# A rewritten order of work up to block d in a fused SSD and squared-ReLU kernel

## The chip, the core and the metric

One core of a Trainium2 chip runs the whole program. Its engines are TensorE (PE), VectorE (DVE), ScalarE (ACT), GpSimd (POOL) and SyncE (SP); each takes its instructions strictly in the order in which the kernel lists them for it. SP, ACT and POOL also issue the transfers between HBM and the core's memory. The metric is the device time of one execution in microseconds (us). The kernel before took 117.4 us, the median of three runs (115.73 to 117.66).

## What is computed

The first part is a chunked state-space recurrence over 4 batches, 8 heads, 768 steps, 32 channels and a state of 16; the second is a feed-forward layer on its result, seen as 3072 tokens of 256 features.

```python
cum = np.cumsum(log_a, axis=-1)                  # in a chunk of 32 steps
L = np.exp(cum[..., :, None] - cum[..., None, :]) * causal
M = np.einsum('bhin,bhjn->bhij', Cc, Bc) * L
y = np.einsum('bhij,bhjd->bhid', M, xc) + np.einsum('bhin,bhnd->bhid', Cc, state) * np.exp(cum)
state = exp(sum(la)) * state + sum_j(B_j x_j exp(cum[-1] - cum_j))
...
h = np.maximum(x @ w_in, 0.0)                    # w_in 256 x 2048
out = (h * h) @ w_out                            # w_out 2048 x 256
```

## The kernel before, in words

The work is cut into 12 units, one for each of 4 batches (b) and 3 stretches of 256 steps (j). Units 0 to 3 are the first stretches of the four batches; units 4 to 11 go on from their states. The result of unit k is a tile `T` of 256 tokens, and block a is the feed-forward layer on unit 0's tokens, block b on unit 1's, and so on to l.

Every step is a token of a hand-written list, `ORDER`, and each engine's queue is simply the order in which the tokens call it. A digit behind the name is the unit, a letter after a colon the engine (`v` DVE, `a` ACT, `p` POOL, `s` SP). The tokens that matter here:

- `id3:512`: three products on constant ones, 512 columns wide (L476), with no use but to keep TensorE busy. `fa`, `la`: the loads of the first and of the later part of `a`. `ldC1:s`, `ldB1:s`, `ldx1:s`: loads of a unit's inputs; `ld4` all three. `wi0` to `wi3`, `wo0` to `wo3`: the weights, a quarter each, cast on the way by POOL's queue (L139, L143). `gB3`: a one-element memset by POOL into the tile of B3, so that the load of B3, and what stands behind it on SP, waits for POOL to come by.
- `sk`, `sp`, `sn`, `p2`: the running products of `a` (clip and scan on DVE, L468 and L469; products on TensorE, L452) for the first and for the later stretches. `pc`, `pb`, `px`: scale C, copy B into the tile `jt`, scale x (L158, L168 or L170, L177). `tr`, `tc`: transpose `jt` on TensorE and copy it back (L195, L208); from unit 4 on `tr` is a transposing transfer issued by SP (L186).
- `mt`: 16 products that give the scores of a unit in PSUM banks 0 to 3 (L220). `mk`: mask one bank on DVE (L229). `sc`: copy one bank on ACT (L234), and `ms` masks that copy on POOL or DVE (L238). `u`: the states (L245), `us` their copy, `z` and `s` (`za`, `sa`, ...) their running sum and its spread form; `sf` is that for the first stretches (L343). `in`, `ina`, `inb`: masked scores times x; `ca`: state times C; `t`: copy of the result to `T`. `rg4` does all of these for a pair of neighbouring units at once.
- `a0` to `a7`: block a's eight first products, each four matmuls and a relu on ACT (L403, L408). `qa0`: the square on DVE (L414). `A0` to `A7`: the second products, four matmuls each into an accumulating bank (L430); the last one is followed by a copy on ACT and a store on SP (L437, L438).

PSUM has eight banks. Six of them go round: the helper `bank()` takes the next in `turn` that is not in `busy`, so which bank a token gets, and whose earlier content must be read before it may write, follows from the list. A first product, a transpose, a unit's states and the scores all draw on these six.

Before, the front is: fillers of 512 columns, `a`, x0, B0, C0, and the loads of units 1 to 3 one behind the other on SP without a pause, since `gB3` stands near the start. The weights come in the order `wi0 wi1 wo0 wi2 wi3 wo1 wo2 wo3`. Blocks a, b and c are mixed with each other and with the units: four first products come before `A0`, products of a and b are still left when unit 3 and block c begin, and 14 groups of products stand between `rg4` and `rg5`.

Of the kernel before, what the change touches and what calls it, by code (L numbers as in the profile page):

```python
# [30 lines left out]
def kernel(  # L31
# [77 lines left out]
    pp = psum.tile([128, 8, 512], FP32, name="pp")  # L109

    def total(i, b, j):
        return 4 * i + b if j == 0 else 8 + 8 * (j - 1) + 4 * i + b
# [223 lines left out]
        else:  # L336
            state[b] = (z, S_d)

    def ph_sd_first(k):
# [3 lines left out]
        nc.vector.tensor_tensor(  # L343
            out=_fap(S_d, 0, [[128, 2], [32, 4], [1, 32]]),
            in0=_fap(pp, v["h"][0] * 512 + 256, [[32, 2], [0, 4], [1, 32]]),
            in1=_fap(Pquad, 4 * total(0, b, 0), [[0, 2], [1, 4], [0, 32]]), op=ALU.mult)
# [87 lines left out]
    def ph_out(blk):  # L434
        b, j = UNITS[blk]
        osb = opool.tile([128, 512], FP32, tag="osb", name=f"osb{blk}")
        nc.scalar.copy(out=osb, in_=pp[:, 6 if blk == 1 else 7, :])  # L437
# [18 lines left out]
    with tc.manual_schedule():  # L456
# [198 lines left out]
        def one(t):  # L655
            f = t.split(":")
            name = f[0].rstrip("0123456789")
            k = int(f[0][len(name):] or 0)
# [13 lines left out]
            {  # L672
                "a": lambda: None,
                "fa": lambda: first_a(k, eng),
                "la": late_a,
                "ldC": lambda: load(k, "C", eng, f[1] if len(f) > 2 else None),
                "ldB": lambda: load(k, "B", eng, f[1] if len(f) > 2 else None),
                "ldx": lambda: load(k, "x", eng, f[1] if len(f) > 2 else None),
                "ld": lambda: load_all(k),
                "gC": lambda: gate(k, "C"), "gB": lambda: gate(k, "B"), "gx": lambda: gate(k, "x"),  # L680
                "afC": lambda: after("C", k), "afB": lambda: after("B", k), "afx": lambda: after("x", k),
                "wi": lambda: load_w_in(k), "wo": lambda: load_w_out(k),
                "id": lambda: idle(k, f[1], dep(f[2]) if len(f) > 2 else None),
                "ef": lambda: eye(eye_f, ones_f), "eb": lambda: eye(eye_b, ones_b[:, 0:128]), "wm": warmed, "hd": head_rows,
                "jz": lambda: eng.memset(jt[k], 0.0), "ti": triangle, "pi": picks, "ku": quads,
                "mb": causal, "pk": picked, "sk": lambda: scan(0), "sp": first_p, "sn": second_scan,
                "su": first_sums, "to": first_total, "fq": first_quad, "p": lambda: second_p(), "pq": second_quad,
                "ps": lambda: A.copy(out=P_sb[:, :, 0:32], in_=P0.rearrange("p (r c) -> p r c", r=2)),  # L688
                "iv": lambda: inv(int(f[1]), int(f[2]), k == 1),
                "pc": lambda: prep_c(k, eng or P, P0 if k == 0 else None),  # L690
                "pb": lambda: prep_b(k, eng or P), "pbl": lambda: prep_b(k, eng, (0,)), "pbh": lambda: prep_b(k, eng, (1,)),
                "px": lambda: prep_x(k, eng or P),
                "tr": lambda: transpose(k, "") if k < 4 else dma_tr(k),
                "trC": lambda: transpose(k, "C"), "trB": lambda: transpose(k, "B"),
                "tc": lambda: trc(k, "", f[1], eng), "tcC": lambda: trc(k, "C", f[1], eng), "tcB": lambda: trc(k, "B", f[1], eng),
                "mt": lambda: scores(k), "mk": lambda: mask_direct(k) if k < 4 else next_mask(k), "sc": lambda: score_copy(k),
                "ms": lambda: mask_copied(k, eng),
                "u": lambda: first_u(k, f[1] if len(f) > 1 else None), "sf": lambda: ph_sd_first(k),
                "ca": lambda: ph_carry(k, live[k]["h"], live[k]["begun"]),
                "in": lambda: intra(k, ""), "ina": lambda: intra(k, "a"), "inb": lambda: intra(k, "b"),  # L700
                "t": lambda: region_t(k, f[1]), "us": lambda: region_us(k),
                "rg": lambda: rg(k), "bk": late_banks, "fr": lambda: busy.discard(4),
                "za": lambda: ph_z(k, 0), "zb": lambda: ph_z(k, 1), "sa": lambda: ph_sd(k, 0), "sb": lambda: ph_sd(k, 1),
            }[name]()
# [59 lines left out]
```

## Time and profile before

| what | value |
|---|---|
| median of three runs | 117.4 us |
| the profiled execution's own time | 116.84 us |
| its span | 115.1 us |
| TensorE busy | 108.9 us, 95% |
| DVE busy | 84.2 us, 73% |
| ACT busy | 76.7 us, 67% |
| POOL busy | 49.8 us, 43% |

The times below are counted from the start of the span. A row of a timeline gives start, length, engine, line, operation, output and inputs, how many were merged, and in brackets how long the engine stood idle before it and what ended that. Lengths of TensorE products overlap, so the distance between starts says more than the length.

### The profile page before, as it was taken

How to read it: one execution, taken by the hardware profiler on the slowest of the kernel's cores; microseconds unless marked ns; L12 is line 12 of the kernel's file. 1: busy time of each engine (PE TensorE's matmuls, PEld its weight loads, DVE VectorE, ACT ScalarE, POOL GpSimd, SP SyncE). 2: the span in 40 equal slices, each digit the busy share in tenths (PEclk: the TensorE clock that was granted, in tenths of full speed). 3: DMA queues.
4: the chain of work that ended last, by engine and by line, in shares of the span. 5: the costliest groups of instructions: out<-in, count | busy, mean ns of one | idle time of the engine just before them, and what ended most of it. 6: DMA issues, size and time to landing. Idle time of an engine off the chain costs nothing.

```text
span 115.1 us, 3998 instructions
## 1 busy us (share of the span) xinstructions
PE 108.9 (95%) x1623; PEld 93.5 (81%) x1623; DVE 84.2 (73%) x187; ACT 76.7 (67%) x161; POOL 49.8 (43%) x102
## 2 busy tenths in 40 slices
PE   7977969999999999999999999999999999999990
PEld 2344749978898989989989989989989899899980
DVE  2469996779599969969965989849668488445530
ACT  0655667865598756787486686786777776876840
POOL 7369972068599457548602669038020020000000
PEclk9999999999999999999999999999999999999999
DMA  1999999989999913935915926623023020020202
GB/s 29 199 196 145 199 203 189 215 167 210 180 191 211 214 24 108 160 89 155 179 46 122 178 97 123 132 95 73 0 100 68 0 100 0 6 91 0 91 0 91
DMA packets 47814, 13.46 MB, mean 117 GB/s; under 512 B 44276, under 2 KB 45876, under 8 KB 47796
## 3 DMA queue, kind: packets, MB, share of 16 engines
q1 hardware_dynamic: 43828, 10.64, 44.8%
q0 software_dynamic: 1664, 2.10, 10.8%
q10 hardware_dynamic: 2304, 0.48, 2.0%
q8 instruction: 12, 0.20, 0.8%
q14 instruction: 6, 0.05, 0.1%
HBM read 10.58 MB, written 3.15 MB: 119 GB/s over the span
## 4 chain that ended last, share of the span: by engine, by line
PE 87%; DMA 6%; POOL 2%; issue 1%; DVE 1%; ACT 1%; ACTq 0%; DVEq 0%
PE pp L430 36%; PE pp L403 36%; PE pp L245 6%; DMA w_out_b<-in_moe_w_out_dram 6%; PE pp L476 4%; PE pp L220 3%; POOL mts L238 1%; PE pp L195 1%; POOL jt L158 1%; PE pp L452 1%; DVE jt L158 0%; DVE Sd L343 0%; ACT bct L208 0%; PE pp L521 0%; ACT osl L722 0%
## 5 line engine op out<-in xcount | busy, mean ns | idle before, releaser
L408 ACT ACTIVATE hb<-pp 128x512 bf16<-128x512 f32 x96 | 55.0, 599 | 24.7 <-PE pp L403 23.1
L430 PE MATMUL pp<-w_out_b,h 128*128 128x256 bf16 (+1 forms) x400 | 54.3, 268 | 0.8 <-DMA w_out_b<-in_moe_w_out_dram 0.8
L414 DVE TENSOR_TENSOR h<-hb 128x512 bf16<-128x512 bf16 x96 | 45.0, 486 | 12.7 <-ACT hb L408 12.3
L403 PE MATMUL pp<-T,w_in_b 128*128 128x256 bf16 x384 | 54.2, 273 | 0.0
L403 PEld LDWEIGHTS <-w_in_b 128*128 128x128 bf16 x384 | 41.4, 114 | 2.2 <-issue 1.0
L430 PEld LDWEIGHTS <-h 128*128 128x128 bf16 x400 | 37.6, 98 | 5.4 <-DVE T L210 1.1
L229 DVE TENSOR_TENSOR mts<-pp,mask 128x512 bf16<-128x512 f32 x45 | 29.6, 677 | 3.3 <-PE pp L220 3.3
L331 POOL TENSOR_TENSOR Sd<-z,Pquad 128x256 bf16<-128x256 f32 x16 | 11.1, 693 | 32.9 <-DVE z L315 25.7
L177 POOL TENSOR_TENSOR xs<-x_nat,Pinv 128x256 bf16<-128x256 f32 (+1 forms) x19 | 14.4, 776 | 5.2 <-DVE Pinv L546 4.6
L158 POOL TENSOR_TENSOR jt<-C_nat,P_sb 128x128 bf16<-128x128 f32 x22 | 9.4, 449 | 1.5 <-ACT P_sb L688 1.0
L476 PE MATMUL pp<-const-bfloat16-1.0 128*128 128x512 bf16 (+2 forms) x19 | 7.3, 516 | 0.8 <-PEq L748 0.8
L315 DVE SCALAR_TENSOR_TENSOR z<-z,Ptot,us 128x64 f32<-128x64 f32 x8 | 2.2, 281 | 6.3 <-ACT us L299 5.4
L437 ACT COPY osb<-pp 128x512 f32<-128x512 f32 x11 | 6.3, 584 | 0.4 <-PE pp L430 0.4
L245 PE MATMUL pp<-mts,xs 64*32 64x128 bf16 x384 | 5.9, 219 | 0.1
L170 POOL CAST jt<-B_nat 128x128 bf16<-128x128 f32 x17 | 5.4, 341 | 1.4 <-DMA B_nat<-in_B_dram 1.4
L220 PE MATMUL pp<-bct 32*64 32x256 bf16 x192 | 5.1, 279 | 0.9 <-DVE bct L210 0.6
L476 PEld LDWEIGHTS <-const-bfloat16-1.0 128*128 128x128 bf16 x19 | 2.2, 122 | 4.0 <-issue 3.7
L245 PEld LDWEIGHTS <-xs 64*32 64x32 bf16 x384 | 4.2, 90 | 0.6 <-issue 0.4
L282 ACT CAST T<-pp 128x512 bf16<-128x512 f32 x7 | 4.1, 592 | 0.4 <-PE pp L245 0.2
L208 ACT CAST T<-pp 128x256 bf16<-128x256 f32 x8 | 2.6, 375 | 2.6 <-PE pp L245 2.6
L245 PE MATMUL pp<-bct,Sd 128*128 128x128 bf16 x40 | 4.2, 220 | 0.0
L220 PEld LDWEIGHTS <-bct 32*64 32x64 bf16 x192 | 2.1, 102 | 2.0 <-issue 0.6
(62 smaller groups left out, 53.4 us busy)
## 6 DMA issues: line engine op xcount, KB each, us to landing
x_nat<-in_x_dram SPq DMA_DIRECT2D x11, 256.0 KB, 3.7
out_dram<-osb SPq DMA_DIRECT2D x11, 256.0 KB, 3.2
B_nat<-in_B_dram SPq DMA_DIRECT2D x11, 128.0 KB, 3.1
C_nat<-in_C_dram SPq DMA_DIRECT2D x11, 128.0 KB, 3.4
w_in_b<-in_moe_w_in_dram POOLq DMA_DIRECT2D x4, 256.0 KB, 6.8
w_out_b<-in_moe_w_out_dram POOLq DMA_DIRECT2D x4, 256.0 KB, 8.2
x_nat<-in_x_dram ACTq DMA_DIRECT2D x2, 128.0 KB, 3.4
bct<-jt SPq DMA_TRANSPOSE x8, 3.6
```

What stands on the lines that cost most here:

```text
L158: eng.tensor_tensor(out=_fap(jt[k % 3], 128 + 144 * g, [[384, 2], [32, 4], [1, 16]]), in0=_fap(loaded[k]["C"], 128 * g, [[16, 2], [32, 4], ...
L177: eng.tensor_tensor(out=_fap(xs, 256 * r, [[256, 2 // n], [32, 8], [1, 32]]), in0=_fap(loaded[k]["x"], 32 * r, [[32, 2 // n], [64, 8], [1, ...
L220: nc.tensor.matmul(pp[64 * u:64 * u + 64, q, r * 256:r * 256 + 256], bct[32 * q:32 * q + 32, r, 0, u * 64:u * 64 + 64], _fap(bct[32 * q:32 ...
L229: nc.vector.tensor_tensor(out=live[k]["mts"][:, q].rearrange("p r g i -> p (r g i)"), in0=pp[:, q, :], in1=mask, op=ALU.mult)
L245: nc.tensor.matmul(dst, w, v, start=bool(need), stop=False, skip_group_check=True, **({} if pos is None else {"tile_position": pos}))
L331: nc.gpsimd.tensor_tensor(out=_fap(S_d, 0, [[128, 2], [32, 4], [1, 32]]), in0=_fap(z, 0, [[32, 2], [0, 4], [1, 32]]), in1=_fap(Pquad, 4 * ...
L403: nc.tensor.matmul(pp[:, h, i * 256:(i + 1) * 256], _fap(w, g * w.shape[2] + (o // 2) * 512 + 2 * (o % 2) + i, [[4, 128]]), T[blk][:, g].r ...
L408: nc.scalar.activation(out=hb.rearrange("p i t -> p (i t)"), in_=pp[:, h, :], func=AF.Relu)
L414: nc.vector.tensor_tensor(out=h2, in0=hb, in1=hb, op=ALU.mult)
L430: nc.tensor.matmul(dst, h2[:, i, r * 128:(r + 1) * 128], w_out_b[gi][:, 2 * o + i, c0:c1], start=first, stop=(fp == 7 and i == 1), skip_gr ...
L437: nc.scalar.copy(out=osb, in_=pp[:, 6 if blk == 1 else 7, :])
L476: nc.tensor.matmul(pp[:, h, 0:int(cols)], ones_b[:, 0:128], ones_b[:, 0:int(cols)] if dep is None else dep, start=True, stop=True, skip_gr ...
```

## The change

The list is rewritten up to the token `D0`; from there on it is unchanged. In the new list `a`, C0, B0 and x0 are loaded in this order, then unit 1, then the later part of `a`. The fillers are 128 columns wide, 51 in all, 24 of them ahead of the first real product. Weights come in turn: `wi0 wo0 wi1 wo1 wi2 wo2 wi3 wo3`. B2 is gated behind `wo2`, B3 behind `wo3`. Unit 1 has two of its four scores copied by ACT, like unit 0, and not masked straight from PSUM. `sf0` and `sf1` become four ACT instructions each. The products of a and b follow one another in their natural order, those of c come after all of a and b, and six groups stand between `rg4` and `rg5`.

```diff
     ORDER = """
-        id3:512 fa1:a la fa0:s ku ef ldx0:h:a eb id2:512 ti id1:512 gB3 pi ldB0:l:a hd ldC0:l:a ldB0:h:s ldC0:h:s
-        ldx0:l:a wm jz0:v mb jz1:v ldB1:s id3:512 sk pbh0:a id2:512 pk pbl0:p wi0 sp pc0:v ldC1:s trB0 wi1 su iv1:0:8
-        trC0 tcC0:0:v tcB0:2:a id1:512 tcC0:1:a ps pb1:a to px0:v jz2:v mt0 id1:512 u0:67 ldx1:s pc1:p fq sc0 mk0
-        id1:512 mk0 ms0:p tr1 tc1:1:v sc0 tc1:0:a sf0 mt1 ldB2:s wo0 ldC2:s ms0:v ldx2:s id1:384 in0 ca0 iv:8:16
-        id3:512 px1:p t0:aa id1:256 mk1 a0 a1 mk1 mk1 mk1 u1 ina1 inb1 sn1 us0 sf1 qa0 a3 ldC3:s wi2 fr p2 wi3 ca1
-        qa1 wo1 pc2 pb2:a t1:vv us1 iv:32:64 a2 zb0 qa2 zb1 A0 ldB3:s wo2 ldx3:s b3 qb3 b0 pq b2 b1 tr2 wo3 sb1 qa3
-        qb0 A1 b5 b4 qb1 qb2 qb5 tc2:1:v qb4 tc2:0:a a5 B0 b6 B1 a7 qa5 iv:16:32 px2 a6 mt2 B3 A2 sc2 u2 b7 us2 pb3:a
-        pc3 mk2 qa6 px3 mk2 A5 ms2:v mk2 ld4 qb6 sf2 a4 qa7 B5 pc4 A6 A3 ld5 pb4 ina2 inb2 tr4 ca2 t2:aa tr3 B4 B2
-        tc3:0:a tc3:1:a u3:45 qb7 ld6 ld7 mt3 qa4 B6 mk3 mk3 mk3 mk3 us3 c4 c5 c0 A4 A7 B7 c6 qc0 za3 qc4 c1 qc5 qc6
-        sa3 px4 qc1 pc5 pb5 bk c2 rg4 tr5 C0 mk4 mk4 qc2 c7 qc7 sb0 c3 qc3 d2 d1 C5 za4 afC2 d0 C1 px5 C4 qd2 zb3 C6
-        C3 qd0 d3 C2 mk4 mk4 C7 px6 sa4 rg5 qd3 sb3 pc6 zb4 sb4 pb6 D0 d4 qd1 tr6 mk5 za5 zb5 sa5 sb5 D1 iv:64:96 mk5
+        id12:128 fa1:a fa0:s ef jz0:v ldC0:l:a ldC0:h:s eb id8:128 ldB0:l:a ldB0:h:s hd ti ldx0:l:s ldx0:h:s ku pi
+        id4:128 sk wm mb jz1:v ldC1:s ldB1:s ldx1:s la sp id4:128 pk id2:128 wi0 pc0:v iv1:0:8 trC0 pbh0:a pbl0:v
+        id3:128 tcC0:0:v tcC0:1:a trB0 su tcB0:2:a ps px0:v iv:8:16 to mt0 fr pc1:p fq u0:67 id12:128 sc0 mk0 mk0 sc0
+        ms0:p ms0:v sf0:a pb1:a ina0 id3:128 inb0 ca0 wo0 t0:av wi1 px1:p tr1 tc1:1:v tc1:0:a us0 id3:128 mt1 mk1 sc1
+        mk1 sc1 a0 ms1:p u1 sf1:a a1 ms1:v ina1 qa0 inb1 ca1 wo1 A0 t1:va us1 qa1 iv:16:32 b0 A1 wi2 jz2:v zb0 zb1 b1
+        a2 qb0 wo2 gB2 ldC2:s ldB2:s ldx2:s a3 qb1 B0 qa2 b2 B1 qa3 b3 qb2 A2 qb3 A3 sn1 B2 sb1 B3 a4 b4 qa4 a5 qb4
+        pc2 pb2:a wi3 b5 qa5 A4 qb5 tr2 tc2:1:v tc2:0:a B4 px2 wo3 gB3 ldC3:s ldB3:s ldx3:s p2 pq A5 iv:32:64 B5 a6
+        mt2 sc2 u2 us2 b6 mk2 qa6 mk2 a7 mk2 ms2:v qb6 sf2 b7 qa7 A6 ld4 qb7 ina2 inb2 B6 ca2 t2:aa pc3 pb3:a px3 A7
+        B7 ld5 c0 c1 qc0 tr3 tc3:0:a tc3:1:a c2 qc1 c3 qc2 u3:45 mt3 C0 pc4 mk3 qc3 C1 pb4 mk3 C2 tr4 mk3 us3 C3 mk3
+        za3 sa3 bk c4 c5 qc4 C4 px4 pc5 pb5 ld6 tr5 ld7 c6 qc5 C5 c7 qc6 rg4 mk4 C6 qc7 sb0 mk4 C7 zb3 sb3 za4 d0 sa4
+        px5 d1 mk4 qd0 d2 mk4 qd1 d3 px6 rg5 qd2 qd3 pc6 zb4 sb4 pb6 D0 d4 tr6 mk5 za5 zb5 sa5 sb5 D1 iv:64:96 mk5 d5
...
-    def ph_sd_first(k):
+    def ph_sd_first(k, eng=None):
...
+        if eng is nc.scalar:
+            for q in range(4):
+                nc.scalar.activation(out=_fap(S_d, 32 * q, [[128, 2], [1, 32]]),
+                                     in_=_fap(pp, v["h"][0] * 512 + 256, [[32, 2], [1, 32]]),
+                                     func=AF.Copy, scale=Pquad[:, total(0, b, 0), q:q + 1])
+            v["S"] = [None, S_d]
+            return
...
-                "u": lambda: first_u(k, f[1] if len(f) > 1 else None), "sf": lambda: ph_sd_first(k),
+                "u": lambda: first_u(k, f[1] if len(f) > 1 else None), "sf": lambda: ph_sd_first(k, eng),
```

More of the change, by code (lines that the diff above doesn't have):

```diff
@@ L59 @@
-        C3 qd0 d3 C2 mk4 mk4 C7 px6 sa4 rg5 qd3 sb3 pc6 zb4 sb4 pb6 D0 d4 qd1 tr6 mk5 za5 zb5 sa5 sb5 D1 iv:64:96 mk5
-        d5 qd4 D2 pb7 d6 qd5 d7 qd6 D3 zb2 e0 qd7 mk5 e1 qe0 sb2 D4 mk5 D5 ld8 pc7 e2 qe1 D6 e3 qe2 px7 D7 rg6 e4 qe3
+        id12:128 fa1:a fa0:s ef jz0:v ldC0:l:a ldC0:h:s eb id8:128 ldB0:l:a ldB0:h:s hd ti ldx0:l:s ldx0:h:s ku pi
+        id4:128 sk wm mb jz1:v ldC1:s ldB1:s ldx1:s la sp id4:128 pk id2:128 wi0 pc0:v iv1:0:8 trC0 pbh0:a pbl0:v
+        id3:128 tcC0:0:v tcC0:1:a trB0 su tcB0:2:a ps px0:v iv:8:16 to mt0 fr pc1:p fq u0:67 id12:128 sc0 mk0 mk0 sc0
@@ L61 @@
+        B7 ld5 c0 c1 qc0 tr3 tc3:0:a tc3:1:a c2 qc1 c3 qc2 u3:45 mt3 C0 pc4 mk3 qc3 C1 pb4 mk3 C2 tr4 mk3 us3 C3 mk3
+        za3 sa3 bk c4 c5 qc4 C4 px4 pc5 pb5 ld6 tr5 ld7 c6 qc5 C5 c7 qc6 rg4 mk4 C6 qc7 sb0 mk4 C7 zb3 sb3 za4 d0 sa4
+        px5 d1 mk4 qd0 d2 mk4 qd1 d3 px6 rg5 qd2 qd3 pc6 zb4 sb4 pb6 D0 d4 tr6 mk5 za5 zb5 sa5 sb5 D1 iv:64:96 mk5 d5
+        qd4 D2 pb7 d6 qd5 d7 qd6 D3 zb2 e0 qd7 mk5 e1 qe0 sb2 D4 mk5 D5 ld8 pc7 e2 qe1 D6 e3 qe2 px7 D7 rg6 e4 qe3
         za6 sa6 tr7 zb6 mk6 e5 qe4 sb6 e6 qe5 e7 qe6 mk6 E0 E1 E2 E3 ld9 px8 mk6 f0 qe7 E4 f1 qf0 pc8 E5 pb8 E6 mk6
```

## The prediction

> **What bounds the kernel now.** I read the page first, then the chain of work that ended last, then each engine's timeline over the first 45 us, because the change rewrites the list only up to the first `D0`; from there both lists are the same. The page, sections 1 and 4:
>
> ```profile
> PE 108.9 (95%) x1623; PEld 93.5 (81%) x1623; DVE 84.2 (73%) x187; ACT 76.7 (67%) x161; POOL 49.8 (43%) x102
> PE 87%; DMA 6%; POOL 2%; issue 1%; DVE 1%; ACT 1%; ACTq 0%; DVEq 0%
> ```
>
> TensorE is the bound: 87% of the last chain. The chain in order of time (start, us, what):
>
> ```profile
> 0.85 4.85 PE pp L476 x11
> 5.70 0.59 PE pp L452 x8
> ...
> 10.33 6.49 DMA w_out_b<-in_moe_w_out_dram
> ...
> 34.87 0.61 PE pp L245 x50
> 35.49 0.35 PE pp L220 x16
> ...
> 36.38 1.75 PE pp L403 x16
> ...
> 43.14 0.55 PE pp L430 x4
> ```
>
> Four lines carry the method. The 0.55 at 43.14 is the first product of `D0`. One group of four products (`a0`, `A0`, ...) costs 1.75/4 = 0.44 us, and after 43.14 there is nothing but such work to the end. So whatever the change does is the shift of `D0`: the time moves one for one with it. TensorE's timeline:
>
> ```profile
> 11.44 0.93 PE L476 MATMUL pp<-const-bfloat16-1.0 128*128 128x512 bf16 x4
> 12.20 1.03 PE L403 MATMUL pp<-T,w_in_b 128*128 128x256 bf16 x8
> ...
> 15.09 0.39 PE L537 MATMUL pp<-pick_p,spread 128*128 128x16 f32 x2 [0.27 <-DVE pick_p L532]
> ...
> 16.96 0.60 PE L430 MATMUL pp<-w_out_b,h 128*128 128x256 bf16 x4 [0.81 <-DMA w_out_b<-in_moe_w_out_dram]
> ```
>
> `a0` starts at 12.20. From there to `D0` the list holds 52 groups (22.7 us), two regions `rg4`, `rg5` of 0.61+0.35 and a little more (2.0), and the transposes, scores and states of units 1 to 3 with `p2` (some 3.6): 28.3 us of work in 30.9, so 2.6 us of stalls, 0.81 of them for `wo0` and 0.27 for `pick_p`. The new list holds the same work. Its `D0` is therefore its `a0`, plus 28.3, plus its stalls.
>
> **The change part by part.** Durations are from these rows, of ACT, DVE and POOL in turn:
>
> ```profile
> 7.94 0.22 ACT L688 COPY P_sb<-pp 128x64 f32<-128x64 f32 x1
> 18.09 2.06 ACT L408 ACTIVATE hb<-pp 128x512 bf16<-128x512 f32 x4 [0.59 <-PE pp L403]
> 21.52 0.48 ACT L208 COPY bct<-pp 128x384 bf16<-128x384 bf16 x1
> 26.32 0.51 ACT L168 CAST jt<-B_nat 128x128 bf16<-128x128 f32 x2
> 28.51 0.65 ACT L208 CAST T<-pp 128x256 bf16<-128x256 f32 x2 [1.18 <-PE pp L245]
> 33.16 1.08 ACT L437 COPY osb<-pp 128x512 f32<-128x512 f32 x2 [0.17 <-PE pp L430]
> ```
>
> ```profile
> 4.68 0.22 DVE L468 TENSOR_SCALAR a_cl<-a_nat 64x128 f32<-64x128 f32 x1 [0.99 <-DMA a_nat<-in_a_dram]
> 4.94 0.42 DVE L469 TENSOR_TENSOR_SCAN cp<-a_cl,const-float32-0.0 64x128 f32<-64x128 f32 x1
> ...
> 10.18 0.41 DVE L343 TENSOR_TENSOR Sd<-pp,Pquad 128x256 bf16<-128x256 f32 x1
> ...
> 18.72 1.14 DVE L414 TENSOR_TENSOR h<-hb 128x512 bf16<-128x512 bf16 x3 [0.57 <-ACT hb L408]
> ...
> 30.51 2.48 DVE L229 TENSOR_TENSOR mts<-pp,mask 128x512 bf16<-128x512 f32 x4 [1.20 <-PE pp L220]
> ```
>
> ```profile
> 5.61 1.64 POOL L139 DMA_DIRECT2D w_in_b<-in_moe_w_in_dram x2 [0.17 <-issue]
> 9.24 1.15 POOL L238 TENSOR_TENSOR mts<-sc,mask 128x512 bf16<-128x512 bf16 x1
> 11.18 1.04 POOL L177 TENSOR_TENSOR xs<-x_nat,Pinv 128x512 bf16<-128x512 f32 x1 [0.24 <-DVE Pinv L546]
> 14.22 0.78 POOL L158 TENSOR_TENSOR jt<-C_nat,P_sb 128x128 bf16<-128x128 f32 x2
> 14.94 0.60 POOL L143 DMA_DIRECT2D w_out_b<-in_moe_w_out_dram x1
> ```
>
> So a relu costs 0.52 in a row of four, a square 0.38, a mask 0.62, two `T` halves 0.65, two output copies 1.08. Loads, by time to landing (from the DMA view, and for `w_in` and `w_out` from their tiles), and the queues' packets and shares of the engines from 5.6 to 8.05 us, from 8 to 10 and from 18 to 22 (q1 is SP's, q0 POOL's):
>
> ```profile
> x_nat<-in_x_dram ACTq DMA_DIRECT2D x2, 128.0 KB, 3.4
> ...
> B_nat<-in_B_dram ACTq DMA_DIRECT2D x1, 64.0 KB, 3.2
> ...
> a_nat<-in_a_dram ACTq DMA_DIRECT2D x1, 16.0 KB, 1.6
> ```
>
> ```profile
> DMA to landing us min/median/max: 5.5/6.8/7.6
> ```
>
> ```profile
> DMA to landing us min/median/max: 6.5/8.2/8.3
> ```
>
> ```profile
> q1 hardware_dynamic: 2733, 0.45, 99.6%
> ...
> q0 software_dynamic: 1, 0.00, 0.2%
> ```
>
> ```profile
> q0 software_dynamic: 261, 0.25, 85.7%
> q1 hardware_dynamic: 624, 0.11, 30.7%
> ```
>
> ```profile
> q0 software_dynamic: 491, 0.75, 105.1%
> q1 hardware_dynamic: 427, 0.05, 15.3%
> ```
>
> Alone, q1 moves 2733/2.45 = 1100 packets per us; beside two weight loads 624/2 = 312; beside four or five 427/4 = 107. POOL issued the first weight load at 5.61, and until 8.05 one weight packet had moved: 2.4 us from issue to first packet.
>
> *Front.* Both halves of `a` are issued first, at 0.8, and land 1.6 later (2.4 against 4.7): the scan ends at 2.4+0.22+0.42 = 3.1. Ahead of the P0 products now stand 24 fillers of 128 columns, not 11 of 512: at the cold rate of 4.85/11/4 = 0.11 us each they last from 0.85 to 3.5, 0.4 too long. P0 starts at 3.5 instead of 5.6. The later fillers stand in stretches where TensorE waits anyway; cost 0. `la` goes back on SP behind nine loads; it lands by 11 and `sn1` wants it near 19: 0. C0 and B0 land 3.2 after issues near 1.2 and 1.8, so hidden too. But x0 is now behind them (issued about 2.3, plus 3.4: 5.7), and C and B are transposed one after the other, so the first scores start at 6.4. Then `sf0` on ACT: four instructions of 0.18 to 0.27 (nearest row 128x64, 0.22), together 0.6 to 1.1, say 0.7, for one DVE instruction of 0.41. `pb1` on ACT waits for B1: issued about 3.6, it meets `wi0` on the engines (issued 3.5, moving from 5.9), and at 312 packets per us its 1024 land near 9.2; bounds 8.0 with no weights in the way, 10 at worst. Behind `pb1` on ACT stand `t0`, `tc1:0` and `us0`; so `tr1` at 9.8, `mt1` at 10.5, **`a0` at 10.9** (10 to 11.7), 1.3 ahead of before.
>
> *Edits with one answer.* The memsets of `jt`, the cast `pbl0` now on DVE and the second half of `t0`, `t1` there stand where DVE waits for a product or a load: 0; if DVE were late there, each is 0.3 to 0.4. `gB3` holds B3 and x3 back until `wo3` is issued at 24.6; behind them on SP stand `ld4` and the stores. x3 lands near 28, `u3` wants it at 33: 0. The order of a and b costs nothing by itself; what it hides less is counted below.
>
> *Unit 1, blocks a and b.* Two of unit 1's masks become ACT copies, one masked by POOL (1.15), one by DVE. Scores can be read 0.5 after `mt1` starts, at 11.05: DVE masks two banks to 11.7 and 12.3, ACT copies two to 11.65 and 12.15 and goes on with relu `a0` (12.7), `sf1` (13.3), relu `a1` (13.85). POOL does `px1` first (x1 landed about 10.4, so to 11.45), then `ms1:p` to 12.8. TensorE: `a0` to 11.35; `u1`, whose banks 0 and 1 were scores, at 11.75; `a1` in bank 2 from 12.35 to 12.8; `inb1` at 13.0; `ca1`, for `sf1`, at 13.35; `A0` at 13.5 (`wo0`, issued at 8.7 on an empty queue, is in by then); `b0`, for `t1`, from 14.2 to 14.65. That is 3.7 for 2.45 of work: stalls 1.25.
>
> Thereafter a, b, A, B flow at 0.44 each, and the weights in turn come 0.5 to 2 us before their use. `tr2` waits for `pb2`, which stands on ACT behind three relus of products just before it: 0.55. `a6` ends at 25.3 and `mt2` at 25.65; `u2` takes the bank of `a6` and waits for its relu (26.1), `b6` the bank that `sc2` empties (26.65), `b7` one of the second mask (27.5): 2.7 for 1.85, stalls 0.85. TensorE reaches `A6` at 28.0.
>
> *wo3.* On POOL `wo1`, `wi2`, `wo2` follow `ms1:p` (12.8 + 0.6 + 0.8 + 0.6), so the gate of B2 opens at 14.9; x2 stands behind B2 on SP. Their 2048 packets share the engines with four weight loads until 21.5. At 107 packets per us some 600 pass by then, at 312 some 1700; the rest go at 1100, so x2 lands between 22.3 and 23.7: I take 23. `px2` (1.04) stands ahead of `wo3` on POOL, so `wo3` is issued at 24.0. The nearest row is the 5.5 of a first `w_in` on an empty queue, which has twice the packets; I take 4.8, bounds 4.2 and 6.5. `A6` at 28.8: stall 0.8 (0 to 3).
>
> The Trainium skill (DMA: Bandwidth & Descriptors, Anatomy of one DMA — SWDGE) gives about 2.0 us plus bytes over 436 GB/s, so an estimate of 2.6 us for the 256 KB of a weight load. By it `wo3` would be there at 26.6, before `A6` is reached, and the sum 0.8 lower. The trace speaks against it: no weight load here came in under 5.5.
>
> *Block c.* Here before has block a and b's products left to mix in; the new list does not. After `ca2` (30.2) ACT has in its queue `t2` 0.65, `pb3` 0.51, two outputs 1.08, four relus 2.06, `tc3:0` 0.48: 4.8 us until relu `c3` (35.2), whose bank `mt3` writes. TensorE has meanwhile A7, B7, c0 to c3, `tr3`, `u3`: 3.1. Stall 1.75. Then C0 to C3 and c4 keep it busy, but `C4` follows `c4` with one group between, and `qc4` waits for relu `c4` and for the last of four masks on DVE: 0.95. `C7` waits for `qc7` behind the first `mk4`: 0.75. Between `rg4` and `rg5` TensorE has six groups (2.6); DVE has four masks 2.5, three squares 1.1 and two small `z`: about 4, and `rg5` needs the last mask and `px5` behind it on POOL: 1.2.
>
> The out stores 0 and 1 now precede `ld5` on SP, which waits for ACT's copies (32.7); C5, B5 still land by 38 and `mt5` is at 46: 0.
>
> *Sum.* 10.9 + 28.3 + 1.25 + 0.55 + 0.85 + 0.8 + 1.75 + 0.95 + 0.75 + 1.2 = 47.3; taking the small overlaps in the last two (TensorE that is late meets fewer waits) 0.4 off: `D0` at 46.9 against 43.1, **+3.8 us**. The profiled execution took 116.84 us, 115.1 of it span; that is 0.5% under the median of 117.4. 116.84 + 3.8 = 120.6.
>
> **The rivals.**
> *Faster:* the earlier front is kept, because ACT and DVE run far enough ahead that no bank and no square is late after `tr2`: `D0` at 10.9+28.3+1.25+0.55 = 41.0, 2.1 before now: 114.7. It decides while the waits after `tr2` stay under 2.1 together; I count 5.9. For it: `a` does land 2.3 earlier and every wait behind it moves along. Against: ACT's rows between `ca2` and `mt3` add to 4.8 however early they begin, since `t2` can't begin before `ca2`. Chance 0.06 for over 2%.
> *Same:* block c's stalls half hidden, because TensorE arrives later than I think and finds ACT ready: 46.9-2.3 gives 118.3. For it: some of my waits overlap. Chance 0.22.
> *Weights late:* x2 starved to the end of `wi3` at 107 packets per us and `wo3` at its row's 6.5: `A6` at 31.5, +2.7: 123.3. For it: 15.3% of the engines for q1 while four weight loads wait. Against: with fewer waiting it had 30.7%. Chance 0.14.
> *Cold clock:* fillers of 512 columns ran at 0.44 us each at first and 0.93 for four at 11.44, so the clock doubled in between, after about 5 us of unbroken work. The new fillers are 51 of 128 columns with gaps. If that does not lift the clock before 10.9, products run at half rate for some 3.4 us: up to +1.7, 122.3. Against: TensorE is busy from 0.85 to 4.6 and most of 4.8 to 8. Chance 0.08. By the Trainium skill (TensorE: Matmul & The Clock Gate, Part 1: The HAM clock gate) the clock doubles after one busy window of about 3.4 us, and the window runs free of the kernel's start; the 0.44 and 0.93 above agree with the doubling, and where the new stretch falls in the window no run here shows yet.
>
> **How the numbers follow.** Forecast 0.50, late weights 0.14, cold clock 0.08: slower by over 2% (above 119.8, about what a measurement of this kernel can tell from no change) 0.72. Same 0.22, faster 0.06. The time is the forecast's, 120.6, its own range 119.5 to 122 (front ±0.7, `wo3` 0 to 3, block c ±1). Taking in the same case at 118.3 and late weights at 123.3, the range is 117.9 to 123.4; outside lie the faster rival and the worst of the late ones, under 2 in 10.
>
> **What would show it.** In the profile of the new kernel: scan done near 3.1 and first scores near 6.4; first L403 at 10.9; an L430 wait for `w_out_b` or a wait through `xs` near 28; idle TensorE before the L220 of unit 3 released by ACT, before an L430 soon after released by DVE, and before the mts products of `rg5`; `D0` near 46.9. It is wrong if TensorE is dense from 30 to 45, or if `a0` starts after 12.

## The result, and the profile after

| | before | after |
|---|---|---|
| median of four runs each, us | 117.0 (115.73 to 117.66) | 126.55 (125.91 to 127.06) |
| the profiled execution, us (its span) | 116.84 (115.1) | 125.91 (124.2) |
| `a0` starts | 12.20 | 14.60 |
| `D0` starts | 43.08 | 52.04 |

The kernel became slower: ratio 1.0853, interval 1.0738 to 1.0967. I had forecast 120.6 and a range to 123.4, so the side was right and the size was not. The profiled execution grew by 9.07 us and `D0` moved by 8.96: the method held, and the whole question is why `D0` is 5.1 later than the 46.9 I gave it. A run over 1.5% above the fastest of its kernel is left out of the ratios but not of the medians, and since the profiled executions of e2, e3 and e10 below are such runs, their landmarks count only where another kernel shows the same.

The page of the new kernel, sections 1, 2 (two lines) and 4. Its lines of code stand 7 further down than before (relu L415, first products L410, second products L437).

```profile
PE 111.5 (90%) x1655; PEld 97.1 (78%) x1655; DVE 83.2 (67%) x185; ACT 80.1 (65%) x172; POOL 50.1 (40%) x102
...
PE   7944979998797797899999999999999999999990
...
PEclk9995599999999999999999999999999999999999
...
PE 62%; DMA 16%; POOL 6%; DVE 5%; ACT 4%; issue 2%; SPq 2%; POOLq 0%; ACTq 0%
```

TensorE is idle for 10% of the span instead of 5%, and only 62% of the last chain, against 87%; transfers have 16% of it, POOL 6%. The third line is the granted clock: in the slices from 9.3 to 15.5 us it was half, while in the profile before it was full from 6.46 on. The chain of the new kernel in order of time (start, length, what) says where the front went:

```profile
3.38 5.50 DMA C_nat<-in_C_dram
...
9.03 0.76 POOL jt L158 x2
9.79 0.21 POOL Pquad L534
...
10.02 0.94 ACT Sd L345 x4
...
11.00 0.61 PE pp L245 x12
...
18.93 9.16 DMA x_nat<-in_x_dram
...
28.17 0.50 POOL xs L177
...
29.17 0.61 POOL w_out_b L143
```

The load of C1 takes 5.50 us. POOL needs it for `pc1` (L158), and behind `pc1` in POOL's queue stands `fq`, which makes `Pquad`; `sf0` on ACT (L345) needs that, and unit 0's own products (L245) need `sf0`. So unit 0, whose last input had landed at 6.25, waits for unit 1's C. POOL's timeline, and the granted clock by stretches (columns: stretch, length, busy PE, PEld, DVE, ACT, POOL, clock, DMA share, GB/s):

```profile
3.47 0.91 POOL L139 DMA_DIRECT2D w_in_b<-in_moe_w_in_dram  x1
9.03 0.76 POOL L158 TENSOR_TENSOR jt<-C_nat,P_sb 128x128 bf16<-128x128 f32 x2 [4.65 <-DMA C_nat<-in_C_dram]
...
9.95 1.14 POOL L238 TENSOR_TENSOR mts<-sc,mask 128x512 bf16<-128x512 bf16 x1
```

```profile
5.60:9.00 3.40, 2.08 (x50) 1.57 (x49) 2.33 (x5) 1.96 (x6) 0.00 (x0) 1.00 1.06 165
9.00:15.80 6.80, 4.67 (x82) 2.93 (x81) 1.88 (x4) 3.39 (x12) 4.79 (x8) 0.50 0.76 125
15.80:20.00 4.20, 3.46 (x73) 2.90 (x59) 3.44 (x10) 3.22 (x11) 3.02 (x6) 0.99 0.59 80
```

POOL stood 4.65 us. TensorE was busy for 2.08 of the 3.40 us before 9.0, and then came 6.8 us at half clock. TensorE's timeline has the rest:

```profile
11.00 0.61 PE L245 MATMUL pp<-mts,xs 64*32 64x128 bf16 x16 [2.83 <-ACT Sd L345]
...
14.60 1.04 PE L410 MATMUL pp<-T,w_in_b 128*128 128x256 bf16 x4
...
17.18 0.47 PE L245 MATMUL pp<-mts,xs 64*32 64x128 bf16 x32 [0.54 <-ACT Sd L345]
...
33.16 0.60 PE L437 MATMUL pp<-w_out_b,h 128*128 128x256 bf16 x4 [0.78 <-DMA w_out_b<-in_moe_w_out_dram]
...
39.05 0.26 PE L220 MATMUL pp<-bct 32*64 32x256 bf16 x1 [0.23 <-ACT hb L415]
39.54 0.42 PE L220 MATMUL pp<-bct 32*64 32x256 bf16 x14 [0.22 <-ACT hb L415]
...
43.77 0.61 PE L437 MATMUL pp<-w_out_b,h 128*128 128x256 bf16 x4 [1.04 <-DVE h L421]
...
47.86 0.61 PE L437 MATMUL pp<-w_out_b,h 128*128 128x256 bf16 x4 [0.65 <-DVE h L421]
...
51.25 0.22 PE L245 MATMUL pp<-xs,jt 64*32 64x64 bf16 x8 [0.20 <-POOL xs L177]
```

The first two rows are the front: 2.83 us of waiting, then a first product at half rate (1.04 where 0.60 is the length at full rate). The others are most of the waits that the prediction named one by one. Counted as the distance between two starts beyond a product's usual pace, as in the last table below, these waits add to 8.6 us. `a0` to `D0` is 37.44 us (before 30.88): some 6.0 more of waits than before and some 0.5 of half clock. The 9.07 are thus 2.4 ahead of `a0`, 6.6 behind it, and 0.1 after `D0`.

### The profile page after: what moved, and what is told of

The parts are those of the page before. It is cut to its first block, busy times and chain, and to the rows that moved or that the text cites. A ratio compares the mean times of both kernels' runs of the same rounds, so it can differ in the third digit from the quotient of the medians.

```text
span 124.2 us, 4067 instructions
## 1 busy us (share of the span) xinstructions
PE 111.5 (90%) x1655; PEld 97.1 (78%) x1655; DVE 83.2 (67%) x185; ACT 80.1 (65%) x172; POOL 50.1 (40%) x102
## 4 chain that ended last, share of the span: by engine, by line
PE 62%; DMA 16%; POOL 6%; DVE 5%; ACT 4%; issue 2%; SPq 2%; POOLq 0%; ACTq 0%
PE pp L437 26%; PE pp L410 25%; DMA x_nat<-in_x_dram 7%; PE pp L245 6%; DMA C_nat<-in_C_dram 4%; DMA B_nat<-in_B_dram 4%; PE pp L220 3%; DVE mts L229 3%; SPq L125 2%; POOL xs L177 1%; POOL w_out_b L143 1%; DVE h L421 1%; ACT hb L415 1%; POOL mts L238 1%; ACT Sd L345 1%
## 5 line engine op out<-in xcount | busy, mean ns | idle before, releaser
L415 ACT ACTIVATE hb<-pp 128x512 bf16<-128x512 f32 x96 | 55.4, 600 | 26.9 <-PE pp L410 25.4
L421 DVE TENSOR_TENSOR h<-hb 128x512 bf16<-128x512 bf16 x96 | 45.9, 493 | 18.3 <-ACT hb L415 17.9
L437 PE MATMUL pp<-w_out_b,h 128*128 128x256 bf16 (+1 forms) x400 | 54.6, 268 | 2.5 <-DVE h L421 1.7
L410 PE MATMUL pp<-T,w_in_b 128*128 128x256 bf16 x384 | 54.9, 274 | 0.5 <-ACT sc L234 0.2
L410 PEld LDWEIGHTS <-w_in_b 128*128 128x128 bf16 x384 | 41.5, 114 | 3.3 <-issue 1.8
L437 PEld LDWEIGHTS <-h 128*128 128x128 bf16 x400 | 37.2, 98 | 7.7 <-DVE h L421 2.4
L229 DVE TENSOR_TENSOR mts<-pp,mask 128x512 bf16<-128x512 f32 x43 | 28.6, 679 | 3.9 <-PE pp L220 3.9
L331 POOL TENSOR_TENSOR Sd<-z,Pquad 128x256 bf16<-128x256 f32 x16 | 10.5, 663 | 32.7 <-DVE z L315 22.9
L177 POOL TENSOR_TENSOR xs<-x_nat,Pinv 128x256 bf16<-128x256 f32 (+1 forms) x19 | 14.8, 796 | 11.5 <-DMA x_nat<-in_x_dram 11.5
L158 POOL TENSOR_TENSOR jt<-C_nat,P_sb 128x128 bf16<-128x128 f32 x22 | 9.6, 456 | 4.7 <-DMA C_nat<-in_C_dram 4.7
L245 PE MATMUL pp<-mts,xs 64*32 64x128 bf16 x384 | 6.4, 226 | 3.4 <-ACT Sd L345 3.4
L245 PEld LDWEIGHTS <-xs 64*32 64x32 bf16 x384 | 4.5, 93 | 4.2 <-issue 3.7
L483 PE MATMUL pp<-const-bfloat16-1.0 128*128 128x128 bf16 x51 | 5.9, 290 | 0.8 <-PEq L755 0.8
L220 PE MATMUL pp<-bct 32*64 32x256 bf16 x192 | 5.8, 291 | 0.9 <-ACT hb L415 0.5
L483 PEld LDWEIGHTS <-const-bfloat16-1.0 128*128 128x128 bf16 x51 | 4.7, 134 | 1.1 <-issue 1.0
L208 ACT CAST T<-pp 128x256 bf16<-128x256 f32 x10 | 3.4, 374 | 3.1 <-PE pp L245 3.0
L245 PE MATMUL pp<-bct,Sd 128*128 128x128 bf16 x40 | 4.5, 223 | 0.2 <-POOL xs L177 0.2
L245 PEld LDWEIGHTS <-jt 64*32 64x32 bf16 x160 | 1.9, 90 | 3.3 <-issue 1.1
L245 PE MATMUL pp<-xs,jt 64*32 64x64 bf16 x160 | 3.4, 199 | 1.1 <-DVE xs L177 0.3
```

The lines of the kernel that those rows point to most:

```text
L158: eng.tensor_tensor(out=_fap(jt[k % 3], 128 + 144 * g, [[384, 2], [32, 4], [1, 16]]), in0=_fap(loaded[k]["C"], 128 * g, [[16, 2], [32, 4], ...
L177: eng.tensor_tensor(out=_fap(xs, 256 * r, [[256, 2 // n], [32, 8], [1, 32]]), in0=_fap(loaded[k]["x"], 32 * r, [[32, 2 // n], [64, 8], [1, ...
L220: nc.tensor.matmul(pp[64 * u:64 * u + 64, q, r * 256:r * 256 + 256], bct[32 * q:32 * q + 32, r, 0, u * 64:u * 64 + 64], _fap(bct[32 * q:32 ...
L229: nc.vector.tensor_tensor(out=live[k]["mts"][:, q].rearrange("p r g i -> p (r g i)"), in0=pp[:, q, :], in1=mask, op=ALU.mult)
L245: nc.tensor.matmul(dst, w, v, start=bool(need), stop=False, skip_group_check=True, **({} if pos is None else {"tile_position": pos}))
L331: nc.gpsimd.tensor_tensor(out=_fap(S_d, 0, [[128, 2], [32, 4], [1, 32]]), in0=_fap(z, 0, [[32, 2], [0, 4], [1, 32]]), in1=_fap(Pquad, 4 * ...
```

## The experiments

Theory A: the 5.1 us beyond the forecast are a front that waits for C1, since `wi0` is issued 2 us earlier than before and its packets hold C1, B1 and x1 up, POOL's queue hands the wait on to unit 0, and idle TensorE loses its clock. Theory B: the narrow fillers fail to lift the clock, whatever the loads do. Theory C: the gates of B2 and B3 set the end, through `wo3`. For what lies behind `a0`, theory D: the order of products, by ACT's and DVE's queues.

**e1: `wi0` behind unit 1's C (A).**

```diff
- id2:128 wi0 pc0:v ... fr pc1:p fq u0:67
+ id2:128 pc0:v ... fr pc1:p wi0 fq u0:67
```

> wi0 is issued behind pc1 on POOL and not ahead of it. If the early weight load is what holds back C1 (it landed at 8.9 in the changed kernel, 2.4 later than I had put it), C1 lands near 6.8, pc1 starts there and not at 9.0, the first intra products at about 8.7 and not 11.0, TensorE never stands idle for over a microsecond before block a, and its clock is not halved. wi0 then lands near 13, so a0 starts at 13.1 at the full clock: 1.5 to 2.5 us less than the changed kernel. Rival: C1 is late by its own place on SP, behind x0. Then it lands at 8.9 again, wi0 later still, and the kernel is 1 us slower or more.

126.21 us, ratio 1.0682 (1.0558 to 1.0805). C1 landed at 7.27, B1 at 8.05, x1 at 9.31; in the changed kernel 8.88, 10.19, 11.30. The queues' packets from 6 to 8 us, first of the changed kernel, then of e1:

```profile
q0 software_dynamic: 218, 0.21, 76.0%
q1 hardware_dynamic: 459, 0.06, 21.6%
```

```profile
q1 hardware_dynamic: 1803, 0.34, 117.6%
```

With one weight load moving (q0), SP's queue (q1) moves 459 packets in 2 us, without it 1803: the collision is shown. But `a0` came only to 13.90. POOL's timeline of e1:

```profile
7.41 0.76 POOL L158 TENSOR_TENSOR jt<-C_nat,P_sb 128x128 bf16<-128x128 f32 x2 [3.71 <-DMA C_nat<-in_C_dram]
8.12 0.91 POOL L139 DMA_DIRECT2D w_in_b<-in_moe_w_in_dram  x1
9.05 0.25 POOL L534 TENSOR_TENSOR Pquad<-Ptot,quad 128x32 f32<-128x32 f32 x1
```

My own edit put the 0.91 of the weight's issue ahead of `fq`, so unit 0 started at 10.31, after a wait of 1.52 for `Sd`, and the clock was halved from 7.49 to 14.31 all the same. The stretches of e1:

```profile
4.08:7.49 3.41, 2.51 (x54) 1.70 (x52) 2.13 (x8) 2.33 (x8) 0.08 (x1) 1.00 1.17 183
7.49:10.90 3.41, 1.89 (x29) 1.52 (x29) 1.29 (x3) 1.49 (x7) 3.39 (x6) 0.50 0.94 140
```

The clock fell at 7.49 and that wait began only at 8.79, so the wait for C1 is not needed for the fall: it came here behind a stretch of narrow products with gaps between them. Half of theory A is shown, its last step is not, and a gain of 1.5 or more was missed.

**e2: no gates (C).** `gB2` and `gB3` taken out.

> The gates of B2 and B3 are left out, so SP issues the loads of units 2 and 3 without waiting for POOL. If the gates cost time, px2 does not wait 6 us for x2, wo3 (behind px2 on POOL) is issued some 3 us earlier, the wait of 0.8 before A6 is gone, and the whole is 1 to 2 us faster than the changed kernel. Rival: the gates pay, since the loads would take the engines from the weights; then L437 products wait for w_out_b or L410 products for w_in_b near 15 to 25 us and the time is the same or up to 2 us longer.

125.82 us, ratio 1.0728 (1.0639 to 1.0816), an interval that overlaps that of the change. Nothing decided; e7 repeats it on a better front.

**e3: wide fillers in the gap (A against B).** Twelve fillers behind `u0` 512 columns wide.

```diff
- u0:67 id12:128 sc0
+ u0:67 id12:512 sc0
```

> Only the twelve fillers behind u0 are 512 columns wide again, so TensorE is busy from 7.3 to about 9.9 where it stood idle from 8.2 to 11.0. If the halved clock from 9.0 to 15.9 is the fillers' doing, the granted clock stays at 1.0, the products between 11 and 16 run at the full rate, a0 starts near 13.9, and the kernel is 0.7 to 1.5 us faster. Rival: these products wait for ACT, DVE and POOL anyway; the clock stays up and the time is the same within 0.3.

124.7 us, ratio 1.0603 (1.049 to 1.0716), below the change's interval. The stretches of e3, and the same stretch of the changed kernel:

```profile
9.00:16.20 7.20, 4.72 (x103) 2.95 (x107) 3.16 (x6) 4.85 (x17) 6.24 (x10) 1.00 0.80 133
```

```profile
9.00:16.20 7.20, 4.90 (x84) 3.19 (x84) 2.28 (x5) 3.79 (x13) 5.19 (x8) 0.53 0.72 119
```

Unit 0's products start as late as before (11.16 for 11.00), but `a0` follows 2.38 later and not 3.60; e5 below, with the same fillers, has 2.37. A full clock is worth 1.2 us up to `a0`; the whole edit gains 1.9 in the medians. It did not keep the clock for good: in this execution it was half from 16.25 to 19.66.

**e4: `fq` ahead of `pc1` on POOL.**

```diff
- fr pc1:p fq u0:67
+ fr fq pc1:p u0:67
```

> fq (0.23 us) stands ahead of pc1 on POOL, so sf0 on ACT no longer waits for C1 through POOL's queue. If sf0 is what held the first intra products (they start 0.05 after it ends), they start near 8.3 and not 11.0; but the POOL mask ms0 still stands behind pc1, so the second half, and a0 with it, moves little: 0.2 to 0.6 us faster, of which some through a clock that stays up. Rival: the intra products wait for something else, the start stays at 11.0.

126.24 us, ratio 1.0756 (1.0658 to 1.0854): no gain that can be told. TensorE's timeline of e4:

```profile
7.40 1.46 PE L483 MATMUL pp<-const-bfloat16-1.0 128*128 128x128 bf16 x12
9.05 0.62 PE L245 MATMUL pp<-mts,xs 64*32 64x128 bf16 x16 [0.19 <-ACT Sd L345]
```

Unit 0 starts 1.95 us earlier and `a0` at 13.12, so POOL's order is a cause; but in this execution the clock was half until 19.89 (twelve fillers in 1.46; 0.88 at full rate) and `D0` came at 52.48. TensorE waited only 0.19 before unit 0's products, so here the low clock, as theory B has it, needs no wait for C1. The two must be mended together.

**e5: both, with `ms0` ahead of `pc1` as well.**

```diff
- fr pc1:p fq u0:67 id12:128 sc0 mk0 mk0 sc0 ms0:p ms0:v
+ fr fq u0:67 id12:512 sc0 mk0 mk0 sc0 ms0:p pc1:p ms0:v
```

> In the changed kernel, fq and ms0 stand ahead of pc1 on POOL, so only unit 1's own scaling waits for C1; and the twelve fillers behind u0 are 512 wide as in e3_fill512. If POOL's queue behind the late C1 is what moved block a, a0 starts near 12 (14.6 in the changed kernel), b0 near 15.5 (18.3), and the clock holds for most of the stretch: 2 to 3.5 us faster than the changed kernel, 123 to 124.5. Rival: a0 is bound by B1, which lands at 10.2 and feeds the cast that stands on ACT ahead of t0; then a0 starts at 13 or later and only the clock's share, about 1, is won.

124.51 us, ratio 1.0693 (1.06 to 1.0787); not to be told from e3 by time, and the interval still meets that of the change, though each of its five runs is below each of the change's four. The profile shows the front. POOL and TensorE of e5:

```profile
8.97 0.76 POOL L158 TENSOR_TENSOR jt<-C_nat,P_sb 128x128 bf16<-128x128 f32 x2 [0.51 <-DMA C_nat<-in_C_dram]
```

```profile
9.95 0.40 PE L245 MATMUL pp<-mts,xs 64*32 64x128 bf16 x16
...
12.32 0.63 PE L410 MATMUL pp<-T,w_in_b 128*128 128x256 bf16 x4
...
14.91 0.47 PE L245 MATMUL pp<-mts,xs 64*32 64x128 bf16 x32 [0.53 <-ACT Sd L345]
```

POOL's wait falls from 4.65 to 0.51, and `a0` stands at 12.32, with full clock. Of the 1.4 that still part it from my 10.9, B1 at 10.11 for 9.2 is the most; e1 puts that down to `wi0`. Behind `a0` little changed: 36.93 to `D0`, 0.5 less than in the changed kernel, about what the half clock had cost there. `A6` (29.91) did not wait for `wo3`, which landed at 28.78 with the gates in place.

**e6: two second products kept for unit 3 (D).** e5, with A7 and B7 held back to cover the wait before unit 3's scores; B6 moves behind `px3`.

```diff
- inb2 B6 ca2 t2:aa pc3 pb3:a px3 A7 B7 ld5 c0 ... u3:45 mt3
+ inb2 ca2 t2:aa pc3 pb3:a px3 B6 ld5 c0 ... u3:45 A7 B7 mt3
```

> e5_pool_order, and B6, A7, B7 are held back: B6 stands behind t2, A7 and B7 (with their output copies on ACT) between u3 and mt3. If the scores of unit 3 wait for ACT's queue between ca2 and relu c3, that queue is 1.1 shorter and TensorE has 0.9 of work where it waited: the wait before the scores falls from about 1.6 to under 0.6, and the kernel is 1.0 to 1.5 us faster than e5_pool_order. Rival: the wait is for something else (a bank, xs3), or the wait comes back before C4: within 0.4 of e5_pool_order.

123.44 us, ratio 1.0502 (1.0375 to 1.0628), an interval that just meets that of e5. TensorE of e6 at unit 3:

```profile
36.12 0.64 PE L220 MATMUL pp<-bct 32*64 32x256 bf16 x16
```

The scores go in one piece where the changed kernel had three with waits; from them to `D0` it is 12.71 us for 13.49.

**e7: e5 without the gates (C).**

> e5_pool_order without the two gates. If the gates hold wo3 back through x2 and px2, wo3 is in before A6 and px3 is not late: 0.7 to 1.5 us faster than e5_pool_order. Rival: without them the loads take the engines from the weights, products of blocks a and b wait for w_in_b or w_out_b, and the time is the same or longer by up to 1.5.

125.38 us, ratio 1.0738 (1.0644 to 1.0832), the interval of e5 overlapping: no gain. `wo3` came at 27.56 and `A6` did not wait for it, but it did not in e5 either, and `a0` to `D0` took 37.96 for e5's 36.93. (`a0` itself stood at 13.56 for 12.32, which is not the gates' doing: the clock was half until 9.65, the twelve wide fillers took 3.89 us for 2.80, and unit 0 started behind them at 11.19.) TensorE, DVE and POOL of e7:

```profile
22.50 1.48 PE L437 MATMUL pp<-w_out_b,h 128*128 128x256 bf16 x12 [0.68 <-DVE h L421]
```

```profile
19.43 3.69 DVE L421 TENSOR_TENSOR h<-hb 128x512 bf16<-128x512 bf16 x5 [0.45 <-ACT hb L415]
...
22.37 0.75 DVE L421 TENSOR_TENSOR h<-hb 128x512 bf16<-128x512 bf16 x2
```

```profile
19.42 0.94 POOL L158 TENSOR_TENSOR jt<-C_nat,P_sb 128x128 bf16<-128x128 f32 x2
...
21.09 1.06 POOL L177 TENSOR_TENSOR xs<-x_nat,Pinv 128x512 bf16<-128x512 f32 x1
```

Without the gate x2 is there earlier, so `px2` (L177) follows `pc2` (L158) on POOL amid DVE's squares: five took 3.69 us, 0.74 each, where the page of the changed kernel has a mean of 0.49 over all 96. The last two of the five, in a second view of the same row, came when `px2` had ended and took 0.75 together. So the edit made a new wait of 0.68 and removed none: the 0.78 for `wo3` stands in the changed kernel's profile, but not in those of e1, e4, e5, e6 and e9, which keep the gates. Theory C falls.

**e8: the old kernel, all fillers 128 wide (B).**

> The kernel before, all its fillers 128 columns wide and nothing else. If narrow fillers do not keep TensorE busy enough, its clock stays at half past 6.5, into block a or to about 14 to 20 us, and the time is 1.5 to 3 us longer than before. Rival: the real work lifts the clock soon enough; P0 starts a little earlier and the time is the same within 0.5.

117.63 us, ratio 1.0062 (1.0014 to 1.0109). The clock was half until 16.36 in its profile and `a0` came at 13.37, yet the whole costs 0.6%. As a cause of 8.5% theory B falls; my expectation of its size was too high.

**e9: e6, with more products mixed (D).** A5 behind `mt2`, B5 behind `u2`, C2 and C3 behind `c4` and `c5`, `c6` ahead of C4, `d0` ahead of C7.

```diff
- ... C1 pb4 mk3 C2 tr4 mk3 us3 C3 mk3 za3 sa3 bk c4 c5 qc4 C4 px4 pc5 pb5 ld6 tr5 ld7 c6 qc5 ...
+ ... C1 pb4 mk3 tr4 mk3 us3 mk3 za3 sa3 bk c4 C2 c5 C3 qc4 c6 C4 px4 pc5 pb5 ld6 tr5 ld7 qc5 ...
```

> e6_hold_a7_b7, and more products held back to stand where TensorE waited: A5 behind mt2, B5 behind u2, C2 and C3 behind c4 and c5, c6 ahead of C4, d0 ahead of C7. If the order of the products is what costs the time between a0 and D0 (6.0 of 36.9 us in e5_pool_order), at least 2 of it goes: D0 is 33.5 to 34.8 after a0, and the kernel is 1 to 2 us faster than e6_hold_a7_b7, near 121.5. Rival: ACT and DVE are simply full from 25 us on, and each wait comes back at the next product; then within 0.5 of e6_hold_a7_b7.

122.42 us, ratio 1.0432 (1.036 to 1.0504), below e5's interval but not clear of e6's. TensorE of e9 before C4 and C7:

```profile
40.41 1.15 PE L437 MATMUL pp<-w_out_b,h 128*128 128x256 bf16 x8 [0.17 <-DVE h L421]
...
44.24 0.61 PE L437 MATMUL pp<-w_out_b,h 128*128 128x256 bf16 x4 [0.22 <-DVE h L421]
...
47.62 0.22 PE L245 MATMUL pp<-xs,jt 64*32 64x64 bf16 x8 [0.35 <-POOL xs L177]
```

The waits for squares shrink from 1.04 and 0.65 to 0.17 and 0.22, and from unit 3's scores to `D0` it is 12.09. I expected 33.5 to 34.8 from `a0` to `D0` and got 36.0: part comes back before `rg5`, where `xs` is now later than TensorE, and in this execution the clock was half from 15.04 to 18.45.

**e10: the spread `sf0`, `sf1` on DVE again.** e5 with `sf0` and `sf1` for `sf0:a` and `sf1:a`.

> e5_pool_order with sf0 and sf1 as one DVE instruction each, as before. If the four ACT instructions cost time, the wait of 0.7 before unit 1's intra products shrinks by half and relu a1 comes 0.4 sooner: 0.3 to 0.8 faster than e5_pool_order. Rival: DVE has the masks of unit 1 in its queue, so sf1 delays ms1 there: the same within 0.3, or up to 0.4 slower.

124.4 us, ratio 1.0532 (1.0438 to 1.0626), overlapping e5's. In its one profile the 0.53 wait for `Sd` before unit 1's products is gone, which no other kernel repeats; the time cannot be told from e5's.

**e11: the old kernel, `wo0` earlier.** The one thing in the new order that looked good, an early `wo0`, put into the old one.

```diff
- trB0 wi1 su ... ldB2:s wo0 ldC2:s
+ trB0 wi1 wo0 su ... ldB2:s ldC2:s
```

> The kernel before, with wo0 issued right behind wi1 (about 7.3 and not 10.3), in a gap in which POOL waits for P_sb. If its landing at 16.8 is what TensorE waits for (0.98 lost), A0 starts by 16 and the kernel is 0.5 to 0.9 us faster than before. Rival: the early load takes the engines from x1 and the second w_in as wi0 did in the changed kernel; x1 lands later, unit 1 is late, and the time is the same or up to 0.8 longer.

116.44 us, ratio 0.9944 (0.9908 to 0.9979): better than both kernels, by little. `A0` of e11:

```profile
15.38 0.60 PE L430 MATMUL pp<-w_out_b,h 128*128 128x256 bf16 x4
```

It starts at 15.38 without a wait; before, at 16.96 after 0.81 for `wo0`.

**e12: the old kernel, `wi0` 2 us earlier (A).**

```diff
- gB3 pi ldB0:l:a ... pbl0:p wi0 sp
+ gB3 pi wi0 ldB0:l:a ... pbl0:p sp
```

> The kernel before, with wi0 issued at 3.7 and not at 5.6, as early as in the changed kernel. If an early weight load holds the units' inputs back, C0, B1 and C1 land 1 to 2 us later, the scores of unit 0 or 1 start later, and the kernel is 0.3 to 1.5 us slower. Rival: by then the inputs of unit 0 are on their way and the weights gain what the inputs lose: the same within 0.3, or faster, as wo0 follows sooner.

119.52 us, ratio 1.0173 (1.0102 to 1.0243). C1 lands at 10.44 (before 7.62), x1 at 12.61 (10.76). POOL of e12, and TensorE before unit 1's transposes:

```profile
10.58 0.76 POOL L158 TENSOR_TENSOR jt<-C_nat,P_sb 128x128 bf16<-128x128 f32 x2 [4.02 <-DMA C_nat<-in_C_dram]
...
11.04 0.76 PE L195 MATMUL pp<-eye_b,jt 128*128 128x128 bf16 x5 [0.42 <-POOL jt L158]
```

POOL waits for C1 as in the changed kernel, the clock is at half from 12.88 to 16.30, `a0` comes at 15.21, `D0` 1.9 later: the collision costs in the other kernel too, by 1.7%.

## Why the prediction was right or wrong, point by point

| step | predicted | measured |
|---|---|---|
| first scores | 6.4 | 6.34 |
| B1 lands | 9.2 | 10.19 |
| unit 0's products | not reckoned | 11.00 |
| `a0` | 10.9 | 14.60 |
| waits, unit 1 | 1.25 | 1.54 |
| `tr2` | 0.55 | 0.45 |
| `u2`, `b6`, `b7` | 0.85 | 1.01 |
| `A6` for `wo3` | 0.8 | 0.94 |
| unit 3's scores | 1.75 | 1.88 |
| C4, C7 | 0.95, 0.75 | 1.21, 0.82 |
| `rg5` | 1.2 | 0.78 |
| `a0` to `D0` | 36.0 | 37.44 |

**The step that failed** is the front: "`pb1` on ACT waits for B1: issued about 3.6, it meets `wi0` on the engines (issued 3.5, moving from 5.9), and at 312 packets per us its 1024 land near 9.2 [...] so `tr1` at 9.8, `mt1` at 10.5, **`a0` at 10.9**". Three things were wrong in it. First, I saw the collision and let it fall on B1 alone; C1 stands ahead of B1 on the same queue, and its packets wait as well. Second, I looked for who waits for B1 (ACT) and not for who waits for C1: POOL, and on POOL's queue `fq` and `ms0`, on which unit 0 hangs. e4 and e5 show it: with `fq` ahead of `pc1` unit 0 starts 1.95 earlier, and in e5, with `ms0` ahead as well and wide fillers that run until then, 1.05. Third, I let TensorE wait there at no price. e3 and e5 show the price of the low clock that went with it: 1.2 up to `a0`. These put `a0` 3.7 later than forecast; the other 1.4 of the 5.1 lie behind it, 0.5 of half clock, 0.5 of waits larger than reckoned, and the 0.4 that I took off for overlap.

**The cold clock** was a rival at 0.08, with "up to +1.7". Its size was right (1.2 to `a0` and some 0.5 behind it). I laid it to 51 narrow fillers with gaps and argued against it that TensorE is "busy from 0.85 to 4.6 and most of 4.8 to 8". It was, 3.65 of 3.75 us and 2.71 of 3.20, and that did not keep the clock. In the changed kernel the fall at 9.02 has 0.8 us of the wait for C1 ahead of it, and that wait, from 8.2 to 11.0, which I did not have in my timeline, fills the first 2.0 us of the half-rate time that follows. But in e1 the clock fell before the wait, and in e4 it stayed half with hardly any wait. So narrow fillers and the wait both have a part, and how much each has in the changed kernel stays open.

**Behind `a0`** every named wait was there, at its place and with the releaser that I named (only that in unit 1 `sf1` held up `ina1` already and not first `ca1`); their sum is 8.63 us, predicted 8.1 with 0.4 taken off for overlap. There was no overlap to take. The faster rival and the same-time rival thus fell as reckoned: ACT's and DVE's queues were late after `tr2` however late TensorE came. e6 and e9 show that the order of the products is the cause of three of the waits (unit 3's scores, C4, C7), since other products put there remove or shrink them.

**wo3** came right by two errors that cancel in part: its issue was to be at 24.0, 13.1 after `a0`, and was at 29.17, 14.6 after it, since x2, gated, took 9.16 from issue; and it landed 3.95 after issue, not 4.8. Late weights as I had them (+2.7) did not come.

**What of the loss is mended by what** (ratios): the front's fillers and POOL order take it from 1.0853 to 1.0693, unit 3's cover to 1.0502, the further mixing to 1.0432. The intervals of neighbours meet, so the single steps are not told apart; the change is clear of e6, and e5 of e9. Of the 5 us left nearly all lie behind `a0`, which e9 has at 12.40 for 12.20 before, while `a0` to `D0` is 36.0 for 30.88. By its profile they are the waits at unit 1, `tr2`, `ina2` and `rg5`, smaller ones, and the stretch of half clock; `wo3` is not among them. I have not removed these one by one, so their shares stay argued.

## What to carry to other kernels

When a transfer will be late, list every instruction that waits for it and, for each, all that stands behind it on its engine's queue: here a copy for the next unit stood ahead of the few small operations that the present unit needed. Price an idle TensorE twice, once as waiting and once as the half-rate stretch that may follow. The distance from one landmark to the point where the lists become equal can be forecast wait by wait; the landmark itself needs the same care.
